# Two transfers of a head pair's rows merged into one, heads paired as neighbours, and a new fixed order of all work

## The chip, the cores and the metric

The kernel runs on one core of a Trainium2 chip. The metric is the device time of one execution in microseconds (us). Each time given as a kernel's time is the median of several executions; the profile is of one execution and has a time of its own.

A core has five engines with queues of their own: TensorE (PE, matrix products and transposes; its weight loads are listed as PEld), VectorE (DVE), ScalarE (ACT), GpSimd (POOL) and SyncE (SP), which here does nothing but start transfers. Sixteen DMA engines carry all transfers. Each engine runs its instructions in the order of the program and waits at the first whose inputs are not ready.

## The reference, cut to what matters

There are two stages. The first is a linear attention with a state matrix for each head, over four sequences (batch) of 768 steps, 8 heads of 40:

```python
for t in range(S):
    y[:, :, t] = np.einsum('bhd,bhde->bhe', rt, state)
    Sa = np.einsum('bhde,bhe->bhd', state, at)
    state_decay = state * wt[:, :, None, :] - np.einsum('bhd,bhe->bhde', Sa, bt)
    state = state_decay + np.einsum('bhd,bhe->bhde', vt, kt)
```

Its output, with the heads side by side as 320 features (x), goes through a mixer over the sequence:

```python
theta = x @ w_theta
zr = x * np.cos(theta)
zi = x * np.sin(theta)
y = np.einsum('ts,bsd->btd', w_tok_r, zr) + np.einsum('ts,bsd->btd', w_tok_i, zi)
u = x + y
out = u + np.maximum(u @ w_ch, 0.0)
```

All inputs and the output are float32. Inside, the products are of bfloat16 operands.

## The kernel before, in words

**Tiles.** A sequence is cut into 6 chunks of 128 steps, and 4 sequences give 24 tiles, numbered i = 0 to 23; six of them in a row (one sequence) share a running state. A tile holds 128 steps in the partitions and 8 heads x 40 features in the row.

**Loads.** For each tile SP loads w, k, b and a (L381), 160 KB each, with steps in the partitions: a run in DRAM is 40 floats, 160 bytes. From tile 8 on v is loaded in the same way. For r, and for v of tiles 0 to 7 (in the code "o"), two tiles are loaded together in another shape (L393): eight steps of one head lie in DRAM as one run of 320 floats, so a partition takes such runs, and the PE turns them later into the transposed form that is needed (`turn_runs`, L500 and L504). These come in two transfers of 160 KB for a pair of tiles, one for heads 0 to 3 (c = 0) and one for heads 4 to 7 (c = 1). So a partition holds one run of head g and one of head g + 4, and heads g and g + 4 are a pair everywhere in the kernel: each PE transpose and each product over 80 columns treats a pair.

To put the other inputs in the same order of heads, they are read through `natural`, "p (c g) d -> p g c d", wherever they are first used: the logarithm of w on ACT (`ln`, L423), the products with k, b and a (`kb` and `ah`, L406 on DVE or L407 on POOL), and the cast of v (L412 or L413). At the other end, `ex` (L730) writes x on DVE back in the order "(c g) d".

**Attention of one tile.** `prep` makes the cumulative logarithms (`cs`, L430 to L436), their exponentials ex and we, the scaled k, b and a, and their transposes (`tkb`, `ta`; L364). `attention_scores` makes three of the 128 x 128 score matrices of all heads (`spsi`, `sphi`, `slv`; L528), each masked while it is copied out of PSUM: on DVE with a product (L538), or on ACT with a copy (L540), after which POOL sets the upper part to zero (`sel`, L542). `recurrence` has the chain from tile to tile: x0 (L569, L575), nx, nu (L587), the new state sum `gt` (L608) and its update on DVE (`egt`), from tile 4 on followed by a product on POOL (`wgt`, L623). `readout` makes the fourth score matrix (`slu`), y (L714 to L723) and x.

**Mixer.** `theta` (L652, L684, L694), then the sines on ACT (L769) for three tiles at a time, then z = x * cos and x * sin, two for each tile (`z`, L783 on DVE, L784 on POOL), then 12 matmuls for each row of tiles (`row`, L797), the sum u (L804) and the last product and sum (`channels`, L820), and the store by SP (`st`, L823). The mixer of one sequence overlaps with the attention of the next. The mixer's weights come by POOL's own transfers (`wdma`: w_theta and w_ch at L831, the token weights in 12 transfers at L857), and are transposed on PE (`wt`, L865).

**Order.** All of this is first recorded as a list of operations, each with its engine, what it reads and what it writes. No scheduler runs when the kernel is built: the list `ORDER` gives the sequence in which the operations are issued, `HOMES` the PSUM bank of each result, and `PICK` names operations that take their alternative engine (for instance DVE to ACT for a mask, POOL to DVE for a product). `WARM` puts a number of matmuls on constant data (L916) ahead of certain operations. SP's queue holds only loads and stores, in the order of `ORDER`; a load into a buffer waits until its last reader is done (4 buffers for w, for k with b, 5 for a, 2 pairs for r, 3 pairs for v), and a store waits for its result while the loads behind it wait too.

Of the kernel before, what the change touches and what calls it, by code (L numbers as in the profile page):

```python
# [11 lines left out]
AF = mybir.ActivationFunctionType  # L12
# [195 lines left out]
def kernel(  # L208
# [14 lines left out]
    nc = tc.nc  # L223
    B, H, S, D = r.shape
# [729 lines left out]
```

## Time and profile before

| what | value |
|---|---|
| median of 3 executions | 205.8 us |
| lowest and highest | 205.5 and 206.66 us |
| the profiled execution | 206.66 us |
| its span from first to last instruction | 204.9 us |
| granted TensorE clock, mean | 0.996 |
| moved by DMA | 30.82 MB in 127,013 packets, 117,632 of them under 512 B |
| a load of w, k, b or a, from issue to landing (median) | 4.0 to 4.2 us |
| a half of r, from issue to landing (median) | 3.5 us |

The page counts an engine as busy while one of its instructions runs; on TensorE, whose matmuls overlap, such a share says less than the number of steps does. A wait that ended an engine's idle time is put down to the engine or transfer that came last. "Idle before" in a row of a group is the time in which the engine did nothing just before these instructions. DMA in the slices is the mean busy share of the 16 DMA engines.

SP waits most in the run for stores (46.5 us before L823, while `oo` on DVE is not ready), and its other waits are short.

### The profile page before, as it was taken

To read this page: it belongs to the slowest core of one execution; us is meant where nothing else is said; L and a number is where in the kernel's file an instruction comes from. 1 tells how busy PE (TensorE), PEld (TensorE's weight loads), DVE (VectorE), ACT (ScalarE), POOL (GpSimd) and SP (SyncE) were. 2 spreads that over 40 slices of the span, in tenths; PEclk is the share of its full clock that TensorE was granted. 3 is DMA by queue.
4 is the path that set the end of the run, shared out by engine and by line. 5 is a ranking of instruction groups with operands and counts; after the bars stand their busy time and mean duration, and the time that the engine had idled before them with its cause. 6 is when DMAs were issued, how large, how long until landed. Compare 5 with 4: busy or idle time off the path is not lost.

```text
span 204.9 us, 8167 instructions
## 1 busy us (share of the span) xinstructions
PE 189.9 (93%) x3376; PEld 153.4 (75%) x3376; DVE 169.2 (83%) x263; ACT 155.9 (76%) x346; POOL 140.3 (68%) x200
## 2 busy tenths in 40 slices
PE   7778879999779999989999999999999999999992
PEld 6566768878568788868878888888888878785761
DVE  5398789999988899968789889989999987778243
ACT  3758658799969989979897788999999957585011
POOL 8266637689679999856879958888399991348000
PEclk9999999999999999999999999999999999999998
DMA  5999899989989999946999799888999700101113
GB/s 127 194 170 202 125 191 203 189 152 207 222 155 178 183 153 223 190 64 111 197 188 192 128 215 187 179 140 158 192 187 182 215 23 3 64 5 69 62 64 128
DMA packets 127013, 30.82 MB, mean 150 GB/s; under 512 B 117632, under 2 KB 126976, under 8 KB 126976
## 3 DMA queue, kind: packets, MB, share of 16 engines
q1 hardware_dynamic: 124544, 27.54, 67.1%
q0 software_dynamic: 2432, 2.77, 8.5%
q8 instruction: 26, 0.43, 0.8%
q14 instruction: 11, 0.09, 0.1%
HBM read 29.13 MB, written 3.93 MB: 161 GB/s over the span
## 4 chain that ended last, share of the span: by engine, by line
PE 64%; SPq 12%; ACT 8%; POOL 7%; DMA 4%; issue 3%; DVE 1%; ACTq 0%; DVEq 0%; POOLq 0%
PE ps_s L797 17%; PE ps_s L364 11%; SPq L381 9%; PE ps_d L528 8%; PE ps_s L684 5%; PE ps_s L652 3%; POOL zr L784 3%; SPq L393 3%; DMA raw_kb<-in_k_dram 2%; POOL zi L784 2%; PE ps_s L500 2%; PE ps_s L587 2%; PE ps_s L608 2%; PE ps_s L694 2%; DMA raw_kb<-in_b_dram 2%
## 5 line engine op out<-in xcount | busy, mean ns | idle before, releaser
L407 POOL TENSOR_TENSOR kb<-raw_kb,ex 128x320 bf16<-128x320 f32 x46 | 39.5, 867 | 8.2 <-DMA raw_kb<-in_k_dram 3.4
L797 PE MATMUL ps_s<-zr,wtok_r 128*128 128x320 bf16 x144 | 40.8, 299 | 0.3 <-POOL zr L784 0.3
L797 PE MATMUL ps_s<-zi,wtok_i 128*128 128x320 bf16 x144 | 40.7, 299 | 0.0
L538 DVE TENSOR_TENSOR lamu<-ps_d,mask_p 128x1024 bf16<-128x1024 f32 x23 | 27.9, 1217 | 1.4 <-PE ps_d L528 1.3
L538 DVE TENSOR_TENSOR psi<-ps_d,mask_p 128x1024 bf16<-128x1024 f32 x23 | 28.0, 1217 | 0.6 <-PE ps_d L528 0.5
L538 DVE TENSOR_TENSOR phi<-ps_d,mask_n 128x1024 bf16<-128x1024 f32 x20 | 24.3, 1217 | 0.9 <-PE ps_d L528 0.9
L538 DVE TENSOR_TENSOR lamv<-ps_d,mask_p 128x1024 bf16<-128x1024 f32 x18 | 21.7, 1219 | 1.7 <-PE ps_d L528 1.6
L407 POOL TENSOR_TENSOR ah<-raw_a,we 128x320 bf16<-128x320 f32 x24 | 20.7, 866 | 2.8 <-DMA raw_a<-in_a_dram 2.1
L784 POOL TENSOR_TENSOR zi<-cs,xp 128x320 bf16<-128x320 f32 x20 | 16.2, 819 | 5.8 <-ACT cs L769 5.8
L784 POOL TENSOR_TENSOR zr<-cs,xp 128x320 bf16<-128x320 f32 x20 | 15.9, 807 | 5.3 <-ACT cs L769 5.1
L797 PEld LDWEIGHTS <-wtok_r 128*128 128x128 bf16 x144 | 14.0, 97 | 5.2 <-issue 0.8
L528 PE MATMUL ps_d<-aT,kbT 64*128 64x128 bf16 x384 | 16.9, 217 | 1.1 <-ACT kbT L367 1.0
L804 DVE TENSOR_TENSOR up<-ps_s,xp 128x320 bf16<-128x320 f32 x22 | 10.6, 487 | 7.9 <-PE ps_s L797 7.9
L797 PEld LDWEIGHTS <-wtok_i 128*128 128x128 bf16 x144 | 14.0, 97 | 3.9 <-issue 0.5
L364 PE MATMUL ps_s<-wide,kb 128*128 128x128 bf16 x192 | 14.8, 219 | 2.0 <-POOL kb L407 1.2
L623 POOL TENSOR_TENSOR gt<-sum,ex 128x320 bf16<-128x320 f32 x13 | 9.7, 744 | 9.2 <-DVE sum L619 9.2
L504 ACT COPY rT<-ps_s 128x512 bf16<-128x512 bf16 x24 | 13.5, 592 | 2.9 <-PE ps_s L500 1.7
L721 PE MATMUL ps_s<-kb,lamv 128*128 128x40 bf16 x192 | 14.9, 180 | 0.0
L528 PEld LDWEIGHTS <-kbT 64*128 64x128 bf16 x384 | 11.7, 94 | 4.2 <-ACT kbT L367 1.4
L723 PE MATMUL ps_s<-kb,lamu 128*128 128x40 bf16 x192 | 14.8, 179 | 0.0
L423 ACT ACTIVATE lw<-raw_w 128x320 bf16<-128x320 f32 x24 | 11.3, 476 | 4.0 <-DMA raw_w<-in_w_dram 4.0
L364 PEld LDWEIGHTS <-kb 128*128 128x128 bf16 x192 | 11.5, 97 | 3.4 <-POOL kb L407 1.5
(169 smaller groups left out, 603.1 us busy)
## 6 DMA issues: line engine op xcount, KB each, us to landing
raw_w<-in_w_dram SPq DMA_DIRECT2D x24, 160.0 KB, 4.2
raw_v<-in_v_dram SPq DMA_DIRECT2D x24, 160.0 KB, 3.7
raw_kb<-in_b_dram SPq DMA_DIRECT2D x24, 160.0 KB, 4.1
raw_kb<-in_k_dram SPq DMA_DIRECT2D x24, 160.0 KB, 4.0
raw_a<-in_a_dram SPq DMA_DIRECT2D x24, 160.0 KB, 4.0
raw_r<-in_r_dram SPq DMA_DIRECT2D x24, 160.0 KB, 3.5
out_dram<-oo SPq DMA_DIRECT2D x24, 160.0 KB, 2.6
wrow_r<-in_moe_w_tok_r_dram POOLq DMA_DIRECT2D x6, 192.0 KB, 4.7
```

Source lines behind the costliest of these rows:

```text
L364: nc.tensor.transpose(out=dst[:, c:c + 128], in_=pair(src, g), identity=ident)
L381: lambda dst=dst, src=src: nc.sync.dma_start(out=dst, in_=src),
L407: pool = ("POOL", lambda: nc.gpsimd.tensor_tensor(out=dst, in0=in0, in1=in1, op=ALU.mult))
L423: add("ACT", "ln", i, lambda: nc.scalar.activation(out=paired(lw)[:, :, :, 0:D], in_=natural(raw_w[s4]), func=AF.Ln), 473, [("raw_w", s4)] ...
L504: add("ACT", "e" + nm, i + x, lambda x=x, dst=dst: nc.scalar.copy(out=dst.rearrange("p (g t q) -> p g t q", g=G, q=8), in_=ps(pr).bitcast( ...
L528: nc.tensor.matmul(t[:, q, g, :], lhsT=lhs[rows(q), g * 128:(g + 1) * 128], rhs=rhs[rows(q), g * 128:(g + 1) * 128], start=True, stop=True)
L538: add("DVE", kindm, i, lambda: nc.vector.tensor_tensor(out=flat, in0=whole(), in1=mask.to_broadcast([128, 2 * G, 128]), op=ALU.mult), 1217 ...
L721: nc.tensor.matmul(o, lhsT=lamv[:, p, g, :], rhs=kb[:, 0, h, 0:D], start=first, stop=False, skip_group_check=True)
L723: nc.tensor.matmul(o, lhsT=lamu[:, p, g, :], rhs=kb[:, 1, h, 0:D], start=False, stop=True, skip_group_check=True)
L784: pool = ("POOL", lambda: nc.gpsimd.tensor_tensor(out=dst, in0=in0, in1=in1, op=ALU.mult))
L797: nc.tensor.matmul(ps(pk)[:, 0:DM], lhsT=wtok[nm][:, s, j * 128:(j + 1) * 128], rhs=zs[c][:, s], start=n == 0 and c == 0, stop=n == NT - 1 ...
L804: add("DVE", "uadd", q, lambda: nc.vector.tensor_tensor(out=u, in0=ps(pk)[:, 0:DM], in1=x, op=ALU.add), 488, [pk, x_key(q)], [u_key(q)], a ...
```

## The change

- r and early v of two tiles come in one transfer of 320 KB instead of two of 160 KB: 12 + 4 transfers instead of 24 + 8. The number of operations goes from 1,614 to 1,598. The transfer may be given to ACT's queue (`alts`); in the new `PICK` none is.
- In this transfer a partition holds the runs of heads 2g and 2g + 1, so neighbours are paired. `natural` goes away: w, k, b, a and v are read as "p (g c) d", which is the order in memory, and x is written in it.
- `ORDER`, `HOMES`, `PICK` and `WARM` are new lists. `WARM` has 46 matmuls in three places instead of 42 in five.

```diff
             runs = ap[bi, :, ci * C:(ci + 2) * C, :].rearrange(
-                "(c g) (t q) d -> c t g (q d)", c=2, q=8)
-            for c in range(2):
-                add("SP", "load" + nm, i, lambda c=c, to=raw[s], runs=runs: nc.sync.dma_start(
-                    out=to[:, c], in_=runs[c]), 600, [], [run_key(nm, i, c)], work=520)
+                "h (t q) d -> t h (q d)", q=8)
+            by_act, by_sync = ((e, lambda q=q, to=raw[s], runs=runs: q.dma_start(
+                out=to, in_=runs)) for e, q in (("ACT", nc.scalar), ("SP", nc.sync)))
+            add("SP", "load" + nm, i, by_sync[1], 600, [],
+                [run_key(nm, i, c) for c in range(2)], work=1000, alts=(by_act,))
...
-    def natural(t):
-        return t.rearrange("p (c g) d -> p g c d", c=2)
...
-            out=paired(lw)[:, :, :, 0:D], in_=natural(raw_w[s4]), func=AF.Ln), 473,
+            out=paired(lw)[:, :, :, 0:D], in_=paired(raw_w[s4]), func=AF.Ln), 473,
...
-            product("kb", i, paired(kb[:, j])[:, :, :, 0:D], natural(raw_kb[s4][:, j]), invW,
+            product("kb", i, paired(kb[:, j])[:, :, :, 0:D], paired(raw_kb[s4][:, j]), invW,
...
-        product("ah", i, paired(ah)[:, :, :, 0:D], natural(raw_a[i % NA]), Wi,
+        product("ah", i, paired(ah)[:, :, :, 0:D], paired(raw_a[i % NA]), Wi,
...
-            cast("v", i, paired(vb)[:, :, :, 0:D], natural(raw_v[i % 6]),
+            cast("v", i, paired(vb)[:, :, :, 0:D], paired(raw_v[i % 6]),
...
-            out=x.rearrange("p (c g d) -> p g c d", c=2, g=G),
+            out=x.rearrange("p (g c d) -> p g c d", c=2, g=G),
...
-WARM = {21: 23, 33: 6, 28: 9, 76: 2, 83: 2}
+WARM = {29: 28, 26: 3, 77: 15}
```

The start of SP's queue, which the lists decide ("r0" is r of tiles 0 and 1, "o0" early v of tiles 0 and 1, x2 for two transfers):

```
before: w0 o0x2 b0 k0 a0 w1 r0x2 a1 k1 b1 w3 w2 o2x2 b2 k2 a2 r2x2 w4 b3 a3 k3 w5 o4x2 k4 b4 a4 r4 w6 r4 a5 k5 b5 o6x2 w7 k6 b6 w8 a6 a7 b7 k7
after:  o0 w0 r0 w1 b0 k0 a0 k1 b1 a1 w2 o2 a2 k2 b2 r2 w3 b3 k3 a3 w4 o4 a4 k4 b4 w5 r4 k5 b5 w7 w6 a5 o6 k6 b6 w8 a6 k7 b7 a7 r6
```

The start of POOL's queue ("sel" the zeroing behind a mask made on ACT, "wdma" a weight transfer):

```
before: ah0 r0 ah1 kb1 kb1 o2 kb2 kb2 ah2 r2 wdma0 kb3 wdma0 ah3 kb3 o4 kb4 kb4 ah4 r4
after:  r0 wdma0 wdma0 sel0 kb1 ah1 sel0 o2 ah2 kb2 kb2 kb3 kb3 ah3 o4 ah4 kb4 kb4 r4
```

Between the products `wgt` of tiles 7 and 8, POOL's queue has eight z and one cast of v before, and nine z, one cast of v and one product for tile 10 after. On TensorE the weight transposes of two blocks, y of tile 7 and the `cs` of tile 10 stand ahead of x0 of tile 8 after, and behind it before.

232 rows, old and new, of tables (HOMES, ORDER, PICK) are left out of this document.

## The prediction

> **What bounds the kernel now.** I read the page first, then the windows of ten microseconds, then the chain of waits, the groups by form, and last single instructions and DMA packets of the trace.
>
> ```profile
> PE 189.9 (93%) x3376; PEld 153.4 (75%) x3376; DVE 169.2 (83%) x263; ACT 155.9 (76%) x346; POOL 140.3 (68%) x200
> ...
> PE   7778879999779999989999999999999999999992
> ...
> DMA  5999899989989999946999799888999700101113
> ```
>
> Two things are full: TensorE from about 70 us on, the DMA engines from 5 to 160 us. TensorE's "busy" hides stalls, since its matmuls overlap, so I measured steps: the time from the first matmul of a group to the first of the next, for each kind of group in the trace. With the lower quartile of each kind as its price, all groups (fillers of L916 included) add up to 174.6 us; 1.1 us lie before the first, 25.3 us are stalls above that price, 3.9 us follow the start of the last group: 204.9. The stalls lie at 10 to 20 us (3.6), 20 to 30 (3.6), 30 to 50 (3.0), 50 to 60 (4.2), 60 to 70 (1.5); the 130 us after 70 hold 8.6 together. So the start, up to 70 us, is where an order can win most, and after it TensorE is nearly a straight queue.
>
> ```profile
> 10.00:20.00 10.00, 8.05 (x158) 6.42 (x157) 9.15 (x11) 6.67 (x17) 6.27 (x8) 1.00 0.93 186
> 20.00:30.00 10.00, 7.94 (x162) 6.78 (x161) 7.95 (x12) 5.60 (x15) 4.96 (x7) 1.00 0.91 158
> ...
> 60.00:70.00 10.00, 8.98 (x186) 7.42 (x180) 8.69 (x12) 9.95 (x22) 9.26 (x14) 1.00 0.99 185
> 70.00:80.00 10.00, 9.92 (x202) 8.39 (x196) 9.78 (x15) 8.79 (x21) 9.95 (x15) 1.00 1.01 171
> 120.00:130.00 10.00, 10.00 (x201) 8.19 (x199) 9.46 (x14) 8.45 (x21) 6.37 (x9) 1.00 0.92 172
> 130.00:140.00 10.00, 10.00 (x233) 8.78 (x230) 8.86 (x15) 9.47 (x25) 9.28 (x12) 1.00 0.94 178
> 140.00:150.00 10.00, 10.00 (x189) 8.45 (x187) 9.88 (x15) 9.69 (x20) 5.96 (x10) 1.00 0.88 175
> 150.00:160.00 10.00, 10.00 (x202) 8.34 (x201) 9.71 (x15) 9.28 (x25) 10.00 (x13) 1.00 0.95 191
> ```
>
> Columns: PE, PEld, DVE, ACT, POOL busy, granted clock, DMA share, GB/s. To 30 us only DMA is full, at 60 to 80 us ACT and POOL are, at 120 to 160 us DVE is busy 37.9 of 40. The chain says the same:
>
> ```profile
> 19.46 2.70 SPq L381
> 22.21 5.09 DMA raw_kb<-in_k_dram
> 27.36 0.87 POOL kb L407
> ...
> 59.04 3.71 DMA raw_kb<-in_b_dram
> 62.88 0.86 POOL kb L407
> 63.74 0.68 POOL gt L623
> 64.42 0.76 POOL zr L784
> ...
> 70.81 0.98 POOL gt L623
> ```
>
> Tile 3's k lands at 27.3 us and everything before it is a queue of loads; at 62.9 to 71 us POOL's products set the pace, and the gt of tile 8 is released only after the row of z products.
>
> **The change, part by part.**
>
> *The merged transfers.* 32 transfers become 16 (12 of r, 4 of early v), all still issued by SP. SP's issues take about 0.6 us when not held up, so SP saves 16 x 0.6 = 9.6 us. What it saves on the path is about nothing: the DMA engines are the limit there. A packet of 160 B took 14.8 ns in the trace and one of 1,280 B about 70 ns; over 16 engines a load of w, k, b, a or v is 1,024 x 14.8 / 16 = 0.95 us, a half of r 128 x 70 / 16 = 0.56 us, the merged one 1.12 us. In the built program its rows are still 320 floats long, so the packets stay, and so does their time. If SP were the limit (its issue at 19.46 us took 2.70), it would be worth up to 6 x 0.6 = 3.6 us before 30 us; I take 0. A cast that needs both halves waits for the same last byte as before.
>
> The Trainium skill (DMA: Bandwidth & Descriptors, Anatomy of one DMA) puts a fixed 2.0 us on each DMA, mostly waiting for the write receipt, which taken serially would make 16 fewer worth 32 us as an estimate. The trace disagrees for a queue kept full: the second half of the first v landed 0.50 us after the first.
>
> *The order of loads.* I add packet times in the queue's order. Before, k of tile 3 stands 25th: 17 full loads and 8 halves, 16.15 + 4.48, and w_theta from POOL's queue (352 packets of 83 ns, 1.83) make 22.5 us of DMA work; it landed 4.8 us later than that sum. In the new order tile 3 is complete after 16 full and 4 merged: 15.2 + 4.48 + 1.83 = 21.5, w of tile 4 no longer being ahead. That is 0.95 us earlier, about 26.4. For tile 4 it is 27.4 against 26.4 (w of tile 5 is moved behind): again 0.95. From tile 6 on the sums are equal (36.3 and 36.2). Against this, w_theta now leaves POOL right after the first r, near 7 us instead of 22, ahead of tile 1's last loads: a of tile 1 is expected at 9.84 + 1.83 + 3.7 = 15.4 us, where all of tile 1 had landed by 13.5. Tile 1 has slack for some of it: its x0 started at 18.4 us, behind the transposes of o of tile 2. So bounds -0.95 and +1.5 us (the +1.5: a of tile 1 at 15.4, its product 0.87, a mask 1.09 that now stands behind it and that nu of tile 0 needs, and 2.5 us from there to the state that x0 of tile 1 needs, as from nu of tile 9 at 72.9 to its state at 75.3, against 18.4). I take -0.4, nearer to the loads of tiles 3 and 4, since x0 of tiles 2 to 4 came 5 to 6 us after their last landing.
>
> *Neighbouring heads.* The products read k, b, a and w in one run of 320 instead of 4 x 2 x 40, and x is written in one run.
>
> ```profile
> L407 POOL TENSOR_TENSOR kb<-raw_kb,ex 128x320 bf16<-128x320 f32 x46 | 39.5, 867 | 8.2 <-DMA raw_kb<-in_k_dram 3.4 <-DMA raw_kb<-in_b_dram 2.8 <-PE ps_s L723 0.8
> ...
> L784 POOL TENSOR_TENSOR zr<-cs,xp 128x320 bf16<-128x320 f32 x20 | 15.9, 807 | 5.3 <-ACT cs L769 5.1
> ...
> L623 POOL TENSOR_TENSOR gt<-sum,ex 128x320 bf16<-128x320 f32 x13 | 9.7, 744 | 9.2 <-DVE sum L619 9.2
> ```
>
> No row has this exact form. The nearest are gt (744 ns: padded output, contiguous first input, a broadcast second) and z (807, all contiguous): a product of 867 falls to between 744 and 867, I take 0.78, so -0.09 each. On the path count only those of the stretch in which POOL is full, 60 to 80 us: nine. Bounds -1.1 and 0; I take -0.4, since some of it only opens a gap before a load. On DVE the write of x (484 ns) is already as quick as contiguous adds (487): nothing.
>
> The Trainium skill (GPSIMD Engine Reference, Elementwise side-by-side) says that GpSimd's addresses come from a hardware pattern at no cost per element; by it the products stay at 867 and this term is 0, the sum 204.8.
>
> *Work moved between engines.* By the choices in PICK: DVE loses four masks (1,217 each) and two z, and gains four kbT, five vT and two products; POOL gains four selects (1,094) and two z and loses three casts of r (717) and two products; ACT gains four masks (about 1,030) and three casts (728) and loses four kbT and five vT. With the rows' means DVE is 2.8 us less, ACT 4.0 and POOL 2.1 more over the run. ACT's extra lies ahead of nx of tile 4, where ACT idles 14 of 40 us: hidden. 0, with the places where it is not hidden among the rivals.
>
> *TensorE's order.* The sum of its steps is the same 169.7 us without fillers, and the tail behind y of tile 23 holds the same groups. Ahead of x0 of tile 8 (65.4 us) stand 2.15 us more: four weight transposes, y of tile 7 and a cs. Stalls from 58 to 72 us are 2.0 us; work put there fills them if its data has landed. Bounds -2.0 and 0; I take -0.6, since each group waits in a fixed queue and the weights' transfers landed as late as 58.7 us. Fillers: 46 for 42, under the wait for the first loads: 0.
>
> **Sum.** -0.4 - 0.4 - 0.6 = -1.4 us on a span of 204.9: 203.5. The profiled execution took 206.66, 1.7 around its span; the median of the three is 205.8. So 205.8 - 1.4 = 204.4 us.
>
> **Rivals.**
> 1. *Nothing gained.* The loads and fillers end where DVE and ACT pace the tiles anyway. For: x0 of tiles 2 to 5 follow each other by 6.4 to 7.5 us, more than a tile's 4.9 us of loads. Against: 25 us of stalls are there. 205.8.
> 2. *Slower: the gt of tile 8 on POOL.* Between the gt of tiles 7 and 8 POOL has nine z and a product of tile 10 where it had eight z: 0.75 + 0.87 = 1.6 us more, in the stretch where POOL is the chain, and x0 of tile 9 began 1.0 us after that gt did. 205.8 + 1.6 = 207.4. It decides as soon as that gt begins later than about 71.8 us. Against: TensorE now has six row groups to do ahead of that x0.
> 3. *Slower: DVE at 120 to 160 us.* Between the state updates of tiles 15 and 20 DVE has 29.6 us of work by the rows' means where it had 27.9, and only 2.1 of 40 us idle: up to +1.7, so 207.5. Against: TensorE has channel and row groups in reserve there.
>
> That the change does not do what it says is excluded for the transfers: the built program has 16 of 128 x 2 x 320.
>
> **Numbers.** Forecast 0.45, rival 1 0.20, rival 2 0.20, rival 3 0.15. What this kernel's measurement can tell from no change is about 0.5%, 1.0 us. Faster: nearly all of the forecast and a little of rival 1, 0.46; same 0.21; slower 0.33. Range: the lower bounds, -0.95 - 1.1 - 2.0, give 201.8; upwards the early delay of 1.5 with rival 3's 1.7 gives 209.0. The forecast's own range is 202.5 to 205.2.
>
> **What would show it.** Right: tile 3's last load before 27 us, products on POOL at 750 to 830 ns, less stall from 50 to 72 us, x0 of tile 8 no later than 65.4. Wrong: a of tile 1 after 15 us with x0 of tile 1 after 19.5 us and no catching up by tile 4; products still at 867; gt of tile 8 after 71.8; DVE over 38 of 40 us at 120 to 160 with stalls on TensorE there. What would overturn all of it is a new wait in the full stretch after 70 us, which the order alone does not show.

## The result, and the profile after

| | before | after |
|---|---|---|
| median, 20 executions each, in turn on one chip | 205.63 us | 204.15 us |
| lowest and highest | 204.35 and 207.57 | 203.0 and 207.59 |
| ratio after to before, 95% interval | | 0.9937, 0.991 to 0.9964 |
| the profiled execution and its span | 206.66 and 204.9 | 205.37 and 203.7 |

The kernel is 0.6% faster, about 1.3 to 1.5 us. In some executions of every kernel the time is some per cent longer; medians here are of all executions, ratios of the others alone. These are the page's busy times and its slices of PE and DMA after the change:

```profile
PE 190.4 (93%) x3380; PEld 153.4 (75%) x3380; DVE 166.0 (81%) x263; ACT 159.1 (78%) x349; POOL 142.0 (70%) x201
...
PE   6779999998979999899999999999999999999992
...
DMA  5999999989998899989979997999947200102113
```

The windows of ten microseconds (PE, PEld, DVE, ACT, POOL busy, granted clock, DMA share, GB/s) that answer to those of before:

```profile
10.00:20.00 10.00, 8.41 (x156) 6.76 (x152) 6.95 (x10) 7.22 (x16) 5.90 (x7) 1.00 1.02 197
20.00:30.00 10.00, 9.53 (x189) 7.58 (x187) 9.63 (x14) 8.25 (x21) 5.22 (x8) 1.00 0.98 173
...
120.00:130.00 10.00, 10.00 (x203) 8.16 (x202) 10.00 (x16) 8.68 (x21) 7.91 (x11) 1.00 0.94 181
130.00:140.00 10.00, 10.00 (x216) 8.77 (x214) 9.28 (x14) 8.69 (x25) 7.31 (x10) 1.00 0.94 158
140.00:150.00 10.00, 10.00 (x201) 8.60 (x199) 9.86 (x17) 9.89 (x17) 8.30 (x13) 1.00 0.99 210
150.00:160.00 10.00, 9.95 (x203) 8.17 (x201) 9.78 (x16) 8.82 (x22) 9.72 (x13) 1.00 0.44 103
```

The DMA share from 10 to 30 us is 1.02 and 0.98 where it was 0.93 and 0.91, and TensorE is busy 9.53 of the 10 us from 20 on, where it was 7.94. DVE is busy 38.9 of the 40 us from 120 on, where it was 37.9; TensorE is busy 39.95 of them. The chain of waits (start, length, what) and POOL's row of the products with k and b:

```profile
7.92 5.29 DMA raw_kb<-in_b_dram
...
45.15 5.87 DMA raw_v<-in_v_dram
51.97 5.49 DMA raw_kb<-in_b_dram
57.60 1.70 POOL kb L405 x2
```

```profile
L405 POOL TENSOR_TENSOR kb<-raw_kb,ex 128x320 bf16<-128x320 f32 x45 | 38.4, 868 | 11.7 <-ACT ex L438 9.6
```

The row of queue starts and one late load at 19 to 27 us is gone from the chain. The product takes 868 ns, as before (867).

Tile by tile, from the trace: the last load of tile 3 landed at 24.3 us (before 27.3), that of tile 4 at 30.2 (32.7). The start of x0, after minus before, is +3.8 us for tile 0, +0.4 for tile 1, -1.6 for tile 3, -2.2 for tile 5, -0.7 for tile 8, -2.9 for tile 10, -1.2 for tile 19; the span ends 1.2 us earlier. So about 2 us are won by 45 us and some of it is given back late: TensorE's stalls between 150 and 170 us went from 1.4 to 2.5 us. That tile 3 lands earlier is not yet the reason: a kernel below that gains nothing (e2) has it at 24.6 us.

### The profile page after: what moved, and what is told of

The parts are those of the page before. It is cut to its first block, busy times and chain, and to the rows that moved or that the text cites. A ratio compares the mean times of both kernels' runs of the same rounds, so it can differ in the third digit from the quotient of the medians.

```text
span 203.7 us, 8123 instructions
## 1 busy us (share of the span) xinstructions
PE 190.4 (93%) x3380; PEld 153.4 (75%) x3380; DVE 166.0 (81%) x263; ACT 159.1 (78%) x349; POOL 142.0 (70%) x201
## 4 chain that ended last, share of the span: by engine, by line
PE 58%; DMA 14%; DVE 9%; ACT 6%; POOL 6%; SPq 4%; issue 2%; DVEq 0%; POOLq 0%; ACTq 0%
PE ps_s L795 18%; PE ps_s L364 8%; PE ps_d L526 8%; DMA raw_kb<-in_b_dram 5%; DMA raw_v<-in_v_dram 5%; PE ps_s L682 4%; DMA wch<-in_moe_w_ch_dram 3%; SPq L381 3%; POOL kb L405 3%; PE ps_s L650 2%; DVE lamu L536 2%; ACT cs L767 2%; PE ps_s L692 2%; PE ps_s L498 2%; PE ps_s L585 2%
## 5 line engine op out<-in xcount | busy, mean ns | idle before, releaser
L405 POOL TENSOR_TENSOR kb<-raw_kb,ex 128x320 bf16<-128x320 f32 x45 | 38.4, 868 | 11.7 <-ACT ex L438 9.6
L536 DVE TENSOR_TENSOR lamu<-ps_d,mask_p 128x1024 bf16<-128x1024 f32 x22 | 26.7, 1218 | 2.9 <-PE ps_d L526 2.7
L536 DVE TENSOR_TENSOR psi<-ps_d,mask_p 128x1024 bf16<-128x1024 f32 x21 | 25.6, 1217 | 2.7 <-PE ps_d L526 2.6
L536 DVE TENSOR_TENSOR phi<-ps_d,mask_n 128x1024 bf16<-128x1024 f32 x19 | 23.1, 1217 | 2.1 <-PE ps_d L526 2.0
L405 POOL TENSOR_TENSOR ah<-raw_a,we 128x320 bf16<-128x320 f32 x23 | 19.9, 864 | 3.9 <-ACT we L446 2.5
L526 PEld LDWEIGHTS <-kbT 64*128 64x128 bf16 x384 | 12.3, 94 | 3.7 <-issue 1.6
L719 PE MATMUL ps_s<-kb,lamv 128*128 128x40 bf16 x192 | 14.8, 180 | 0.0
L721 PE MATMUL ps_s<-kb,lamu 128*128 128x40 bf16 x192 | 14.8, 179 | 0.0
L367 ACT COPY uT<-ps_s 128x320 f32<-128x320 f32 (+1 forms) x11 | 4.5, 406 | 12.0 <-PE ps_s L650 12.0
L818 DVE SCALAR_TENSOR_TENSOR oo<-ps_s,up 128x320 f32<-128x320 f32 x22 | 10.0, 485 | 4.4 <-PE ps_s L692 3.8
```

The source lines that it names most:

```text
L405: pool = ("POOL", lambda: nc.gpsimd.tensor_tensor(out=dst, in0=in0, in1=in1, op=ALU.mult))
L526: nc.tensor.matmul(t[:, q, g, :], lhsT=lhs[rows(q), g * 128:(g + 1) * 128], rhs=rhs[rows(q), g * 128:(g + 1) * 128], start=True, stop=True)
L536: add("DVE", kindm, i, lambda: nc.vector.tensor_tensor(out=flat, in0=whole(), in1=mask.to_broadcast([128, 2 * G, 128]), op=ALU.mult), 1217 ...
L719: nc.tensor.matmul(o, lhsT=lamv[:, p, g, :], rhs=kb[:, 0, h, 0:D], start=first, stop=False, skip_group_check=True)
L721: nc.tensor.matmul(o, lhsT=lamu[:, p, g, :], rhs=kb[:, 1, h, 0:D], start=False, stop=True, skip_group_check=True)
L818: add("DVE", "oo", t, lambda ck=ck, u=u, oo=oo: nc.vector.scalar_tensor_tensor(out=oo, in0=ps(ck)[:, 0:DM], scalar=0.0, in1=u, op0=ALU.max ...
```

## The experiments

Each ratio is to the kernel before on the same chip, with its 95% interval; the kernel before took 206.9, 206.8, 206.5 and 206.8 us there in the four sets of runs.

**Merging alone, and the new lists alone.** The first kernel (e1) has the lists of before and merged transfers, the second (e2) the new lists and halves. Both have neighbouring heads, so e2 differs from the changed kernel in the transfers alone, and from the kernel before in the lists and the pairing:

```diff
 # e1: the changed code with before's ORDER, HOMES, PICK and WARM,
 #     each merged load at the place of the first half
 # e2: the changed kernel with
-                "h (t q) d -> t h (q d)", q=8)
+                "(g c) (t q) d -> c t g (q d)", c=2, q=8)
...
+            for c in range(2):
+                add("SP", "load" + nm, i, lambda c=c, to=raw[s], runs=runs: nc.sync.dma_start(
+                    out=to[:, c], in_=runs[c]), 600, [], [run_key(nm, i, c)], work=520)
```

> The merged transfers and neighbouring heads in the old order of everything else (each merged load where the first of its halves stood). Theory A (the gain is the order of the loads and of the other work; the DMA engines are full, so the number of transfers does not matter): same as before, ratio 0.999 to 1.002, k of tile 3 lands at 27 us, POOL products at 867 ns. Theory B (a half keeps the DMA engines for 0.56 us but SP for 0.6 or more, so the engines run dry between halves: DMA share 0.82 to 0.94 at 10 to 25 us before): ratio 0.993 to 0.996, k of tile 3 lands 1.5 to 3 us earlier, DMA share over 0.97 at 10 to 25 us. Theory C (only the whole new order, made for these transfers, gains): 1.00 or slower.

> The new order of everything, but each merged load as two adjacent halves in the same partitions (neighbouring heads kept). Theory A: as the new kernel, ratio to before 0.992 to 0.996. Theory B: the gain is lost or more than lost, ratio 0.998 to 1.004, a of tile 3 lands at 25.5 to 27.5 us instead of 24.3. Theory C: 0.997 to 1.000.

Measured: e1 205.32 us, 0.992 (0.9883 to 0.9957); e2 207.32 us, 1.0012 (0.9964 to 1.006). Merging with the old lists makes the whole gain; the new lists and the pairing without merging make none that shows. In the trace of e1 tile 3 was complete at 24.1 us and x0 of tile 5 began 1.4 us earlier than before (I read that trace only to 50 us, since the granted clock was 0.50 from 57.5 to 61.0 us). In the trace of e2 the halves cost little at first: x0 of tiles 1 to 7 starts 0.6 to 0.7 us later than in the changed kernel. Then tile 8 is complete at 60.8 us instead of 58.4, and its x0 starts 2.4 us later; the granted clock, 0.50 from 58.0 to 61.4 us, may have a part in that. The span ends 1.9 us later.

**The order of the loads, crossed.** e3 is the changed kernel with its first 40 loads in the sequence of before, e4 the kernel before with its first 47 in the new sequence, e10 is e1 with the new sequence:

```diff
 # e3
-o0 w0 r0 w1 b0 k0 a0 k1 b1 a1 w2 ...
+w0 o0 b0 k0 a0 w1 r0 a1 k1 b1 w3 w2 ...
 # e4 (o and r x2), e10
-w0 o0 b0 k0 a0 w1 r0 a1 k1 b1 w3 w2 ...
+o0 w0 r0 w1 b0 k0 a0 k1 b1 a1 w2 ...
```

> The new kernel with the first 40 loads of SP's queue in the order of before (merged), all else new. Theory A: most of the gain is lost, ratio to before 0.998 to 1.003, k of tile 3 lands 1 to 2 us later than 23.7. Theory B: the gain stays, 0.992 to 0.996. Theory C: slower than before, 1.002 to 1.01, since the other queues were laid out for the new loads.

> The kernel before with the first 47 loads of SP's queue in the new order (two halves each, adjacent), all else as before. Theory A: ratio 0.993 to 0.998, tile 3 complete by 26.4 us. Theory B: 0.999 to 1.003. Theory C: 1.000 to 1.01, since TensorE's old order asks for tile 0 first and its loads now come 2 us later.

> Merged transfers, the early loads (up to the load of v of tile 8) in the new order, and all other work in the order of before. The prediction's term for the order of loads was -0.4 us (bounds -0.95 and +1.5) beside nothing for the merging. If the new order of loads is worth that by itself, this is 0.2% below the run with merging alone, 0.990. If it only fits its own order of work, as the two crossed runs suggest (old loads in the new order of work 1.0025, new loads in the old order with halves 1.017), this loses: 1.005 or more, with x0 of tile 1 some 4 to 6 us late, since o of tile 0 and r stand ahead of tile 0's own loads and TensorE, DVE and ACT take their work in an order that does not expect it.

Measured: e3 207.0 us, 1.0025 (0.9986 to 1.0063), x0 of tile 0 at 18.6 us, 7.0 later than before; e4 210.08 us, 1.0172 (1.0119 to 1.0226), x0 of tile 1 6.1 us late; e10 209.21 us, 1.0153 (1.0106 to 1.02), x0 of tile 1 5.1 us late although tile 3 was complete at 23.1 us and tile 8 at 50.8, 5.6 us earlier than before. Loads that land earlier are worth nothing when the other queues take their work in another sequence. In these runs the order of the loads has no price of its own that could be added up.

**Where merging counts.** Halves for the pairs to tile 7 only, and from tile 8 on only:

```diff
+            if i <= 6:      # e5;  e6: if i >= 8
+                halves = ap[bi, :, ci * C:(ci + 2) * C, :].rearrange(
+                    "(g c) (t q) d -> c t g (q d)", c=2, q=8)
...
```

> The changed kernel with only the early merged transfers (o and r of tiles 0 to 7, eight pairs) as two halves again; the eight later transfers of r stay merged. Splitting all 16 cost the whole gain (ratio to before 1.001 where the changed kernel has 0.994). If the gain is made at the start, where SP has to keep the DMA engines fed (theory S: each further transfer takes SP some 0.6 us), this gives 1.000 or a little above, tile 3 complete about 1 us later than 24.3 us and x0 of tile 5 by 1 us or more later. If the gain is made after 45 us (theory L), it gives 0.994 and the start is unchanged but for some tenths.

> The other side: o and r of tiles 0 to 7 merged, the eight transfers of r of tiles 8 to 23 as halves. Theory S: 0.994, as the changed kernel, since x0 of tiles 0 to 7 are the same. Theory L: 1.000 or above, with the loads of tile 8 landing 2 to 4 us later than 58.4 us and x0 of tile 8 over 1 us later than 64.7.

Measured: e5 207.57 us, 1.0042 (1.0001 to 1.0083); e6 207.38 us, 0.9986 (0.9945 to 1.0028). With the changed kernel at 0.9937, splitting the early pairs costs about 1%, and that is clear of the intervals; the late ones cost about 0.5%, which is not (0.9945 against 0.9964). The two don't add up to the loss of e2; the intervals are too wide for that.

**Number or form.** Merged transfers, and behind each of them one (e7) or two (e9) transfers of 160 bytes which nobody reads:

```diff
+            for _ in range(2):      # e7: once
+                add("SP", "tick", i, lambda to=tick[len(ticks):len(ticks) + 1],
+                    src=ap[bi, 0, ci * C:ci * C + 1, :]:
+                    nc.sync.dma_start(out=to, in_=src), 600, [], [("tick", len(ticks))], work=0)
+                ticks.append(i)
```

> All 16 transfers merged, and behind each of them SP issues one more transfer of a single row of 160 bytes that nobody reads: the number of transfers is that of the split form, the bytes and rows of r and v are those of the merged one. If what costs is one more transfer in SP's queue (S, 0.6 us each, 9.6 us in all), the gain goes as it did when all were split: 1.000 to 1.002. If the merged form is carried better by the DMA engines (theory F: longer work for each start, better spread over the 16 engines), the small transfers cost nothing: 0.994, and the DMA share from 10 to 25 us stays at 0.95 to 1.06.

> As the run with one small transfer behind each of the 16 merged ones, now with two. In that run the small transfer took SP 0.46 us and the load behind it 0.37 instead of 0.59, so 0.24 us net, where a second half takes 0.60; it ended at 0.9964 of before, between the changed kernel (0.994) and the one with halves (1.001). Theory S, SP's issuing time counts: two of them cost about 0.5 to 0.7 us for each merged transfer, as much as a second half, and the time goes to 1.000 or 1.001; tile 8 complete 1 to 2 us later than with one. Theory F, the form of the transfer counts and not the number: no more than with one, 0.994 to 0.997.

Measured: e7 206.25 us, 0.9964 (0.9924 to 1.0005); e9 208.04 us, 1.0102 (1.0047 to 1.0158). Two transfers without a load of their own take back all of the gain and more. So it is not the form of the merged transfer: what costs is the number of transfers in SP's queue. That it costs through SP's time was the idea (theory S), and it isn't shown: two small transfers take SP 0.46 and 0.25 us and the load behind them 0.2 us less, together about 0.5 us, less than the 0.60 us of a second half, and should have given 1.000 to 1.001, but cost 3.4 us (1.0102 against 0.9937) where the halves cost 1.5. SP's issues in order of time (start, length, what), first before, then after, each around r of tiles 2 and 3, then e9 there:

```profile
15.33 1.33 SPq L381 DMA_DIRECT2D raw_a<-in_a_dram  x1
16.70 1.46 SPq L393 DMA_DIRECT2D raw_r<-in_r_dram  x2
18.28 0.52 SPq L381 DMA_DIRECT2D raw_w<-in_w_dram  x1
18.84 0.58 SPq L381 DMA_DIRECT2D raw_kb<-in_b_dram  x1
19.46 2.70 SPq L381 DMA_DIRECT2D raw_a<-in_a_dram  x1
```

```profile
15.36 0.99 SPq L381 DMA_DIRECT2D raw_kb<-in_b_dram  x1
16.39 0.68 SPq L392 DMA_DIRECT2D raw_r<-in_r_dram  x1
17.11 0.60 SPq L381 DMA_DIRECT2D raw_w<-in_w_dram  x1
17.76 0.58 SPq L381 DMA_DIRECT2D raw_kb<-in_b_dram  x1
18.39 1.75 SPq L381 DMA_DIRECT2D raw_kb<-in_k_dram  x1
```

```profile
17.01 1.20 SPq L394 DMA_DIRECT2D raw_r<-in_r_dram  x1
18.25 0.75 SPq L400 DMA_DIRECT2D tick<-in_r_dram  x2
19.05 0.39 SPq L383 DMA_DIRECT2D raw_w<-in_w_dram  x1
19.48 0.58 SPq L383 DMA_DIRECT2D raw_kb<-in_b_dram  x1
```

Each issue starts as the one before it ends: to 50 us no pause of SP is longer than 0.12 us in the traces of before, after and e9, with 54 issues in 46.7 us before and 46 in 46.5 us after. A load of 1,024 packets that isn't held up is issued in 0.52 to 0.60 us. Of the 21 issues of 1.3 us or more before and after, 19 begin with more than 2,000 data packets of SP's queue outstanding, counted from the packets' times; so I read them as a full queue, not a slow SP, and SP's unbroken row of issues is no proof that SP is the limit. When the w behind the r was started, 507 packets were outstanding before (18.28 us, behind two halves), 1,408 after (17.11, behind the merged transfer) and 312 in e9 (19.05, behind the two small ones). The halves add 256 packets in 1.46 us of SP's time; in that time 16 engines carry some 1,600 packets of 160 B (14.8 ns each). In e9 the DMA share shows the same between 30 and 45 us, where the changed kernel has 1.01, 0.97 and 0.92:

```profile
30.00:35.00 5.00, 5.00 (x121) 4.49 (x119) 5.00 (x7) 4.11 (x12) 3.27 (x4) 1.00 0.77 157
35.00:40.00 5.00, 4.50 (x100) 3.70 (x98) 4.53 (x7) 4.23 (x10) 2.73 (x3) 1.00 0.86 166
40.00:45.00 5.00, 5.00 (x106) 4.01 (x103) 4.80 (x7) 4.41 (x14) 2.69 (x4) 1.00 0.81 145
```

But the DMA engines' emptiest moments lie elsewhere. The issue of 2.70 us at 19.46 ended when SP's queue had all but run empty, and the trace names no wait for it; the changed kernel has such a moment too, behind a merged transfer whose issue took 1.87 us. First before, then after:

```profile
22.00:22.50 0.50, 0.50 (x13) 0.40 (x12) 0.50 (x2) 0.00 (x0) 0.50 (x2) 1.00 0.09 11
29.50:30.00 0.50, 0.50 (x13) 0.30 (x11) 0.50 (x2) 0.30 (x1) 0.50 (x2) 1.00 0.08 15
```

From 5 to 50 us at most four packets are in flight for 2.4 us before and 2.4 us after, for 1.5 us in e2 and 3.7 us in e9. So the engines' empty time does not put these kernels in the order of their times, and how a further transfer comes to cost some 0.1 us stays open.

**The second half from another queue.** The early pairs as halves, the second of each issued by ACT:

```diff
+                for c, (e, q) in enumerate((("SP", nc.sync), ("ACT", nc.scalar))):
+                    add(e, "load" + nm, i, lambda c=c, q=q, to=raw[s], halves=halves: q.dma_start(
+                        out=to[:, c], in_=halves[c]), 600, [], [run_key(nm, i, c)], work=520)
```

> The eight early pairs as halves, the second half of each issued from ACT's queue at the time at which SP issued the merged one; the later ones merged. SP's queue is as in the changed kernel, the number and form of the transfers are as in the run with the early ones split. Theory S: the time of the changed kernel, 0.994, or up to 0.3% more where ACT is held up by eight issues of about 0.6 us. If each transfer has a price of its own whoever issues it, or if the form counts (F): the same time as the run with the early ones split on SP. It tells nothing if that run loses nothing.

Measured: 209.91 us, 1.0149 (1.0098 to 1.02). All expectations missed, and the reason is a new wait. In this program a transfer waits until the one eight places ahead of it in the order of issue has landed. On SP that had always happened at least 2.0 us earlier (before and after, to 50 us); in e9, where small transfers take some of the eight places, the least margin is 0.24 us, so this wait doesn't explain e9 either. In ACT's queue the transfer stands later than SP's neighbours, and ACT, with all its work behind it, stood still for 4.04 us (start, length, what, and in brackets the idle time and what ended it):

```profile
15.63 0.54 ACTq L393 DMA_DIRECT2D raw_v<-in_v_dram  x1
16.21 0.37 ACT L364 COPY aT<-ps_s 128x256 f32<-128x256 f32 x1 [4.04 <-DMA raw_w<-in_w_dram]
```

x0 of tile 0 came at 20.2 us instead of 15.3. So this run doesn't tell whether freeing SP in this way would do what merging does.

**TensorE's order ahead of x0 of tile 8.** The groups that the change put there, back behind it:

```diff
 # TensorE
-y6 wt8 spsi8 tkb9 wt8 cs10 gd7 sphi8 wt7 y7 wt7 x08 sphi9
+y6 spsi8 tkb9 gd7 sphi8 x08 wt8 wt8 cs10 wt7 y7 wt7 sphi9
 # ACT: the two copies of wt8 behind egd7 and ekb9; one wt8 and one wt7 in other banks
```

> The changed kernel with the four weight transposes of two blocks, y of tile 7 and cs of tile 10 put behind x0 of tile 8 on TensorE, as they stood before (on ACT the two copies of the first block go behind the state copy of tile 7; two results change banks). My prediction gave -0.6 us to their new place (bounds -2.0 and 0): stalls that they fill. If that step holds, stalls of about 0.6 us or more come back between 61 and 66 us ahead of x0 of tile 8, the work behind is late by as much, and the ratio to before goes from 0.994 to 0.997. If they only stood in for one another (rival: TensorE has ready work in any order here), x0 of tile 8 comes earlier by up to their 2.15 us, no stall appears, and the time stays at 0.994; if x0 of tile 8 and what hangs on it were late before, it even falls to 0.990.

Measured: 208.75 us, 1.0171 (1.0106 to 1.0235). x0 of tile 8 began at 64.79 us, no earlier than in the changed kernel (64.66), and x0 of tile 9 at 75.0 instead of 70.8. TensorE's stalls from 60 to 70 us are 4.6 us where they were 0.8 (a part of them is the lower clock below; TensorE is busy 7.7 of these 10 us where it was 9.7). So the 2.15 us of work did fill waiting time. The loss is far more than the 0.997 expected if the step held. The trace shows two more losses: a wait of 0.7 us before a weight transpose, which the moved copies make, and a lower clock. In windows of one microsecond (columns as above):

```profile
55.00:56.00 1.00, 0.52 (x14) 0.32 (x8) 1.00 (x3) 0.00 (x0) 0.72 (x2) 1.00 0.45 71
56.00:57.00 1.00, 0.00 (x0) 0.00 (x0) 1.00 (x2) 0.68 (x2) 1.00 (x2) 1.00 1.00 160
...
59.00:60.00 1.00, 1.00 (x18) 0.88 (x13) 0.06 (x1) 0.98 (x3) 0.13 (x1) 0.50 1.27 228
```

Other executions of this kernel, with a mean clock of 0.995 to 1.0, took 208.5 to 209.4 us, no less than this one's 208.65; what makes up the rest there stays open.

**Stalls taken out one by one.** The changed kernel with four steps moved:

```diff
 # SP
-k8 w10 b9 b8 a9
+k8 w10 b8 b9 a9
 # POOL: b's product of tile 8 ahead of that of tile 9; both pieces of w_ch together
-... w_ch(small) ... wtok v11 ... wtok w_ch(large)
+... w_ch(small) ... w_ch(large) wtok v11 ... wtok
 # ACT
-sin sin ea23
+sin ea23 sin
```

> The changed kernel with four steps moved, nothing else: b of tile 8 loaded ahead of b of tile 9 and multiplied ahead of it on POOL; the larger piece of w_ch issued by POOL next to the smaller one, ahead of two blocks of token weights, instead of behind them; on ACT the copy of a of tile 23 between the two last sines instead of behind them. In its trace TensorE stalls 1.07 us before the transposes of k and b of tile 8 (the b product waits for the load at 58.4), 1.00 us at 84 us for w_ch, and 0.52 us at 162 us for the bank that this copy empties. If TensorE is a straight queue from 60 us on, as I read it, what is removed there comes out at the end: up to 0.8 + 0.9 + 0.4 = 2.1 us less, given back in part where DVE and POOL are full at 140 to 160; I expect 1 to 2 us, a ratio to before of 0.984 to 0.989. If DVE or POOL sets the pace there and the stalls are only where it shows (rival), the ratio stays at 0.993.

Measured: 205.43 us, 0.9956 (0.9925 to 0.9988), no better than the changed kernel. The wait for w_ch is gone (from x0 of tile 11 to the next group 0.34 us instead of 1.34), but stalls of 0.31 and 0.36 us are new at 76 and 79 us. b of tile 8 landed at 58.47 us (58.36 before the move; this execution ran 0.7 us late from the start), since SP's issue of it now took 2.67 us, and the transposes waited 1.52 us instead of 1.07. At 162 us the bank came free earlier, and the next score matrix then waited for the mask that the copy had delayed. So the straight queue is refuted and the ratio is what the rival gave; that the DMA engines, POOL and DVE set what is ready there fits the new waits, but was not tested further.

## Why the prediction was right, and where not

The forecast was 204.4 us and 204.15 came; its sum of -1.4 us is near the measured -1.5, but it is made of the wrong terms. That it came so near is luck.

- *The merged transfers, "I take 0", because "the DMA engines are the limit there".* This step failed. Merging is worth -1.7 us by e1 (0.992 of 206.9) and +1.5 by e2 when it is undone in the changed kernel. The DMA share of 0.93 and 0.91 that I read as full did not make the number of transfers free: e9 adds transfers with almost no bytes and loses 3.4 us. The bound that I wrote down for a limit at SP, -3.6, holds the gain, though that SP's time is the way is not shown. The packets' own time is nearly unchanged, as I had said: 14.9 and 15.0 ns for 160 B, 71 and 75 for 1,280 B to 50 us.
- *The order of loads, -0.4.* Tile 3 was complete earlier by 3.0 us, not 0.95, but merging in the old order does the same (24.1), and so do the new lists with halves (24.6), which gain nothing. a of tile 1 landed at 14.0 us, not 15.4, and x0 of tile 1 at 18.8: that delay stayed small. The crossed runs show no gain from the loads' order alone.
- *Neighbouring heads, -0.4.* Zero: 868 ns against 867. The nearest rows, gt and z, don't bound a product by its address pattern. The Trainium skill (GPSIMD Engine Reference, Elementwise side-by-side) has it that the address pattern costs nothing per element, and the trace agrees.
- *TensorE's order, -0.6.* The groups do fill waiting time, as I had said: moved back, with the copies and banks that go along, they cost 4.8 us of the whole (1.0171 against 0.9937), of which their own 2.15 us of work can explain less than half. As a gain against the kernel before it isn't shown: e1 is as fast without this arrangement. It may only repair what other parts of the new order make worse, such as x0 of tile 0 at 15.3 us instead of 11.6.
- *Work moved between engines, 0.* DVE rose over 38 of 40 us, a sign of rival 3 that I had named, but without stalls on TensorE in that stretch to speak of; about 1 us is given back between 150 and 170 us, and that DVE is the cause isn't shown. Rival 2 fell: the gt of tile 8 began at 69.7 us (70.8 before). Taken together the new lists are worth nothing measurable: the changed kernel (0.991 to 0.9964) and e1 (0.9883 to 0.9957) have overlapping intervals.
- *The fixed 2.0 us of a DMA.* The section of the Trainium skill that I took it from (DMA: Bandwidth & Descriptors, Anatomy of one DMA) gives it for DMAs issued by GpSimd, and these are SP's. Taken serially it made 32 us of 16 transfers; the runs show 1.5 to 1.7 us, some 0.1 us each.

## What to carry to other kernels

A high DMA share doesn't make the number of transfers free. Where one queue issues them without a pause, fewer and larger transfers can gain even though their bytes and packets stay the same; try it by itself, and try the opposite with small transfers that nobody reads. An order tuned as a whole could not be taken apart here: an earlier sequence of loads or a stall removed by hand cost time or gave nothing as long as the other queues kept theirs.

## What the hardware showed that I had not expected

- An issue on SP takes 0.52 to 0.60 us for a load of 1,024 packets, 0.60 for a half of 128, 0.46 for a single row of 160 bytes, and the load behind that row 0.37. Held up, a load's issue took up to 2.7 us before and 2.2 us after, to 50 us.
- In e12, with 1.6 us without a matmul from 55.5 us, TensorE's granted clock was 0.50 from 59.0 to 62.4 us; in e2, with 2.1 us without one from 56.5, it was 0.50 from 58.0 to 61.4 us. In e9 a gap of 2.2 us from 58.4 was not followed by a lower clock, so the length of the gap alone doesn't decide. The Trainium skill (TensorE: Matmul & The Clock Gate, What's actually happening) states that the gate knows only half and full rate, and these two traces agree. The advice of the Trainium skill to avoid idle gaps over about 3 us (TensorE: Matmul & The Clock Gate, Why this matters for your kernels) is too mild here: with these gaps of 1.6 and 2.1 us the half rate came.
